# The start of a spectral-filter and gated-FFN kernel: float32 filters, a shared load queue, and batch 0's spectrum in pairs on one side

## The chip, the cores and the metric

The kernel runs on one core of a Trainium2 chip. The metric is the device time of one execution in microseconds (us). The core's engines are named as the profile names them: PE is TensorE, DVE is VectorE, ACT is ScalarE, POOL is GpSimd, SP is SyncE. Loads that SP or ACT issues and loads that POOL issues stand in different DMA queues.

## The reference

The first half is a filter in frequency, the second a feed-forward block with a gate, on all tokens:

```python
X = np.fft.rfft(x, axis=1)                    # x: 8 x 3008 x 256, float32
Y = X * (filt_r + 1j * filt_i)[None, :, :]    # filters: 1505 x 256, float32
y = np.fft.irfft(Y, n=3008, axis=1).reshape(24064, 256)
gate = np.maximum(y @ w_gate, 0.0)            # w_gate, w_val: 256 x 1536
out = (gate * (y @ w_val)) @ w_out            # w_out: 1536 x 256
```

## The kernel before

The transform over 3008 is done as 94 x 32. For each batch there are six stages. **A**: matmuls in float32 with the table `WA` transform over the 94 (`a_bank`, PSUM tile `psA`). Then VectorE transposes 32x32 blocks (the **turn**, in float32 units of two bf16) so that the 32 lie on the partitions (tile `at`). **Forward** (`fwd`): matmuls with table `F2`, 16 small ones into `psX`; there are six forward steps per batch. **Products** (`product`): `psX` times the real filter (`tt`) and times the imaginary filter (`uu`), for batch 0 on VectorE except three pairs on POOL (`ON_POOL`), for which ScalarE first copies `psX` to `xs`. **Inverse** (`inv`): matmuls with the tables `I2t` and `I2u` into four PSUM tiles `psD`; three inverse steps per batch, each on two forward steps. The result is copied to SBUF as bf16 and turned back. **C** (`item_c`): matmuls with the table `M1` back over the 94, into `psY`, copied to `yT`: 512 tokens of y. From there `gv` and `o_part` do the feed-forward block, 47 blocks of 512 tokens, in twelve steps each.

The order is written by hand: each engine runs its instructions in the order of the program. What is looked at here is the front, before the first `gv`. Batch 0 goes through all stages there, and batch 1's stage A goes between them in sixteen **items** (`item`, `a_1`: one matmul into `psA` and its copy to bf16). Everything of the batches 2 to 7 is placed at numbered steps of the feed-forward loop.

Loads in the front. Batch 0's x (3.08 MB) goes on SP's queue, with a few pieces on ACT's, then the tables `F2` and `tabs`. The filters are loaded by POOL, which casts them to bf16 in the DMA: first the rows of an odd partition, which lie backward in memory (`load_back`, 256 elements each, first half of the groups), then the rows of an even partition, long ones of 3072 elements (L234), then the second halves of the backward rows. The two end rows (`load_own_filters`) come before all these; a small copy on POOL (`hold_gpsimd`) makes POOL wait for a late piece of x before it issues the rest. On SP a tiny load called `hold` reads one element block of the imaginary filter: SP waits there until those filter rows have landed, and only then issues batch 1's x into the buffers of batch 0's x. A DMA on SP's or POOL's queue uses one of eight semaphores, so each also waits for the landing of the one eight before it. After its products POOL issues the weights (`load_vg`, `load_o`), copies `M1`, and multiplies the imaginary filter by the table `conj` for the later batches.

Layout of batch 0's spectrum. The copies of `psD` (L464) write a bf16 tile `DS0` in groups of four: for one column index c, four values that are two neighbours in the 32 and two column halves. The turn (`turn_d`, `turn_pairs`, L306) reads and writes two float32 units that are neighbours. `d_rows` then hands strided columns of `D0` to TensorE as weights.

```python
copy(dst[:, k:k + 3:2, :, g:g + 2].rearrange("p m e f -> p m f e"),   # L464
     psD[c].rearrange("p m (f e) -> p m f e", f=2))
return D0[:, n2 // 2, :, n2 % 2 * 2 + h]                              # d_rows
```

Lines that the text names: L190 x pieces, L234 long filter rows, L241 backward rows, L271 stage A, L283 batch 0's copies of `psA`, L296 the items' copies, L301 batch 1's turns (`turn_a`, single float32 units on both sides), L306 batch 0's turns, L408 forward, L426 and L428 products on POOL and VectorE, L451 inverse, L464 copies of `psD`, L550 `psY`, L567 `gv`, L683 the sign of the imaginary filter. `warm` puts matmuls on a junk tile into TensorE's gaps.

Of the kernel before, what the change touches and what calls it, by code (L numbers as in the profile page):

```python
# [12 lines left out]
FP32 = mybir.dt.float32  # L13
BF16 = mybir.dt.bfloat16
# [15 lines left out]
N1, N2 = 94, 32  # L30
# [5 lines left out]
def _ap(t, offset_elems, ap_list):  # L36
    return dataclasses.replace(
        t, offset=t.offset + offset_elems, ap=[list(p) for p in ap_list]
    )
# [77 lines left out]
def kernel(  # L117
# [50 lines left out]
    AS0 = pro.tile([128, 4, N2 // 2, D // 8, 4], BF16)  # L168
    DS0 = AS0.rearrange("p q n c f -> p (q n c f)").rearrange("p (k c f) -> p k c f", c=D // 2, f=4)
    dCb = consts.tile([128, 48, D], BF16)  # L170
    D0 = dCb[:, 0:32, :].rearrange("p n d -> p (n d)").rearrange("p (k c f) -> p k c f", c=D // 2, f=4)
    AS1 = [dCb[:, 32:48, :].rearrange("p n d -> p (n d)").rearrange("p (l c d) -> p l c d", l=NC2, d=D // 2)]
    WF = consts.tile([128, 4, 32], FP32)
    M1 = consts.tile([128, 2, N1], BF16)
# [2 lines left out]
    I2u = pro.tile([128, 2, NG // 2, 64], BF16)  # L177
    Ftr = consts.tile([128, NG // 2, D], BF16)
    Fti = consts.tile([128, NG // 2, D], BF16)
    WgT = consts.tile([128, 2, DFF], BF16)  # L180
    WvT = consts.tile([128, 2, DFF], BF16)
    WoT = consts.tile([128, NFT, D], BF16)
# [10 lines left out]

    WHOLE = ((0, 0, NX2 * D), (1, 0, NX2 * D))
    H = NG // 2
    FILT = ((filt_r, Ftr), (filt_i, Fti))
    tabs = pro.tile([128, tab_h.shape[1]], BF16, tag="tabs", bufs=1)
    conj32 = pro.tile([128, 2], FP32, tag="conj32", bufs=1)
    perm, conj, own = tabs[:, 0:64], tabs[:, 64:66], tabs[96:, 66:578]
# [15 lines left out]
    def make_back_u():  # L215
        nc.scalar.copy(conj32, conj)
        for r in range(2):
            nc.scalar.mul(I2u[:, r], I2t[:, 1 - r], conj32[:, r:r + 1])
# [7 lines left out]
    def load_filters():  # L226

        for src, dst in FILT:
            for c in range(4):
                load_back(src, dst, c, 0, H // 2)  # L230
        for src, dst in FILT:
            for c in range(4):
                r, k1, n = 32 * c, 1 + H * c, H - c // 3
                nc.gpsimd.dma_start(dst[r:r + 31:2, :n, :], _ap(src, k1 * D, [[N1 * D, 16], [1, n * D]]))  # L234
        for src, dst in FILT:
            for c in range(4):
                load_back(src, dst, c, H // 2, H - c // 3)

    def load_back(src, dst, c, g0, g1):
        r, k1 = 32 * c + 1, 1 + H * c + g0  # L240
        nc.gpsimd.dma_start(dst[r:r + 31:2, g0:g1, :],  # L241
                            _ap(src, (N1 - k1) * D, [[N1 * D, 16], [-D, g1 - g0], [1, D]]))
# [61 lines left out]
    def turn_pairs(dst, src):  # L304

        nc.vector.transpose(dst.bitcast(FP32).rearrange("p k c g -> p c k g"),  # L306
                            src.bitcast(FP32).rearrange("p n c g -> p c n g"))
# [13 lines left out]

    def turn_d(h):

        d = slice(h * D // 4, h * D // 4 + D // 4)
        turn_pairs(D0[:, :, d], DS0[:, :, d])

    def store_half(b):
        w = N2 * D // 2
# [86 lines left out]
    def product(b, i, e, k, pool=False):  # L415

        psX = psXs[b, i, e]
        pool_, bufs, dt = (fs, 3, FP32) if b else (pro, 10, BF16)
        p = pool_.tile([128, 2, D], dt, tag=("tt", "uu")[k], bufs=bufs, name=("tt", "uu")[k])
        filt = (Ftr, Fti)[k][:, 2 * i + e, :]  # L420
        filt = dataclasses.replace(filt, ap=[list(filt.ap[0]), [0, 2], list(filt.ap[1])])
        if pool:
            if not k:
                xs[i] = pro.tile([128, 2, D], FP32, tag="xs", bufs=3, name="xs")
                nc.scalar.copy(xs[i], psX)
            nc.gpsimd.tensor_tensor(p, xs[i], filt, op=ALU.mult)  # L426
        else:
            nc.vector.tensor_tensor(p, psX, filt, op=ALU.mult)  # L428
        tus[b, i, e, k] = p
        left[b, i, e] -= 1  # L430
        if not left[b, i, e]:
            done(psX)
# [8 lines left out]
    def inv(b, q):  # L441

        psD = [bank("psD", 2, D) for c in range(4)]
        last = 0 if b else 1
        for m in range(2):
            for k in range(last + 1):
                for r in range(2):
                    for c in range(4):
                        for e in range(2):
                            i = 2 * q + m  # L450
                            nc.tensor.matmul(psD[c][64 * e:64 * e + 64, m],  # L451
                                             (I2t, I2u)[k][32 * c:32 * c + 32, r, 2 * i + e, :],
                                             tus[b, i, e, k][32 * c:32 * c + 32, r],
                                             start=(k == r == 0), stop=(k == last and r == 1),
                                             tile_position=(32 * c, 64 * e))
        dst = sb.tile([128, 8, D], BF16, tag="dsb", bufs=3, name="dsb") if b else DS0
        def out(cs):
            for c in cs:
                copy = nc.vector.tensor_copy if (c % 2 if b else (q, c) in ((1, 3), (2, 0), (2, 1))) else nc.scalar.copy
                if b:  # L460
                    copy(dst[:, c:8:4, :], psD[c])
                else:
                    k, g = 4 * q + c // 2, c % 2 * 2
                    copy(dst[:, k:k + 3:2, :, g:g + 2].rearrange("p m e f -> p m f e"),  # L464
                         psD[c].rearrange("p m (f e) -> p m f e", f=2))
                done(psD[c])
        if not b:
            return out(range(4))

        def rest():  # L470
            out((2, 3))
            for z in range(4):
                nc.sync.dma_start(_ap(Dbuf[b], (64 * (z // 2) + z % 2) * NG * D + 8 * q * D,
                                      [[2 * NG * D, 32], [1, 8 * D]]),
                                  dst[32 * z:32 * z + 32])
        out((0, 1))
        return rest

    def first_b(item):

        def products(i, es=(1, 0)):
            for e in es:
                for k in range(2):
                    product(0, i, e, k, pool=(i, e) in ON_POOL)

        fwd(0, 0)
        warm(2)
        fwd(0, 1)
        make_back_u()
        for i in range(2):  # L490
            products(i, (1,))
        for k in range(2):
            for i in range(2):
                product(0, i, 0, k)
        warm(2)
        fwd(0, 2)
        products(2)
        warm(1)
        fwd(0, 3)
        products(3, (1,))  # L500
        fwd(0, 4)
        item(2)
        products(3, (0,))
        inv(0, 0)
        fwd(0, 5)
        products(4)
        item(2)
        products(5)
        place_own()
        inv(0, 1)  # L510
        item(1)
        inv(0, 2)

    dCs = {}

    def d_rows(b, n2, h):

        if b:
            return dCs[b, n2 // 8][:, n2 % 8, h * 128:(h + 1) * 128]
        return D0[:, n2 // 2, :, n2 % 2 * 2 + h]  # L520

    def load_d(b):

# [20 lines left out]
    def item_c(k, h):  # L544

        if h == 0:
            yTs[k] = sb.tile([128, 2, W], BF16, tag="yT", bufs=3, name="yT")
        psY = bank("psY", W)
        for (o, b, n2, n1, w) in runs(k * W, W):
            nc.tensor.matmul(psY[:, o:o + w],  # L550
                             d_rows(b, n2, h),
                             M1[:, 1, n1:n1 + w] if b == 0 else M1[:NROW, 0, n1:n1 + w],
                             start=True, stop=True)
        dst = yTs[k][:, h]
        if h == 0 or k:
            nc.scalar.copy(dst, psY)  # L556
        else:
            nc.vector.tensor_copy(dst, psY)
        done(psY)
# [74 lines left out]
    nc.vector.memset(XF[1][:, 0:2 * q], 0.0)  # L634
    nc.gpsimd.memset(XF[1][:, 2 * q:], 0.0)
    load_x(0, both, ((0, q, 2 * q),))
    load_x(0, sp, ((0, 2 * q, 4 * q), (1, 0, 2 * q), (1, 2 * q, 4 * q)))
    nc.sync.dma_start(F2, nc.inline_tensor(f2_h, name="dft_f2").ap())
    nc.sync.dma_start(tabs, nc.inline_tensor(tab_h, name="dft_tab").ap())
    for (src, dst) in FILT:  # L640
# [4 lines left out]

    warm(18, 256)
    new_at(0)
    for n2, h in ((0, 0), (0, 1), (4, 0), (4, 1)):
        a_0(n2, 4, h * D // 2, D // 2)
    for p, dq in ((1, 0), (1, 1), (1, 2), (1, 3), (2, 0), (2, 1), (2, 2), (3, 0), (3, 1), (3, 2), (2, 3), (3, 3)):  # L650
        a_0(NC2 * p, NC2, dq * D // 4, D // 4)
        if p == 3:
            turn_0(dq)
    for r in range(2):
        make_back_t(r)
        warm(4 - 2 * r)
    hold = sb.tile([2, 8], BF16, tag="hold", bufs=1)
    nc.sync.dma_start(hold, Fti[96:98, 4, 0:8])
    load_x(1, sp, ((0, 0, 2 * q), (0, 2 * q, 4 * q), (1, 0, 2 * q), (1, 2 * q, 4 * q)))
    items = iter([(p, s, h) for p in range(4) for h in range(2) for s in range(2)])  # L660

# [10 lines left out]
    load_vg(0, DFF // 2)  # L672
    load_vg(DFF // 2, DFF)
    load_o()
    nc.gpsimd.tensor_copy(M1, tabs[:, 578:].rearrange("p (l n) -> p l n", l=2))
    for h in range(2):
        turn_d(h)
# [2 lines left out]
        item_c(0, hh)  # L680
    item(3)
    turn_1(0)
    nc.gpsimd.tensor_scalar(Fti, Fti, conj[:, 0:1], 1.0, op0=ALU.mult, op1=ALU.mult)  # L683
    nc.sync.dma_start(WF, nc.inline_tensor(fold_h, name="dft_fold").ap())
    prologue.close()
    fs = ctx.enter_context(tc.tile_pool(name="fs", bufs=2))
# [86 lines left out]
```

## Time and profile before

| what | value |
|---|---|
| time, median of 3 runs (lowest, highest) | 874.51 us (873.02, 874.99) |
| the profiled execution: time, its span | 875.37 us, 873.6 us |
| granted TensorE clock over the span | 0.995 |
| busy: PE, DVE, ACT, POOL | 852.4, 579.5, 500.2, 462.3 us |
| DMA: moved, mean rate | 101.61 MB, 116 GB/s |
| batch 0's first `psA` starts, last ends (us) | 5.0, 20.4 |
| first product on DVE | 23.3 |
| SP past the hold, first issue of batch 1's x | 24.7 |
| first item's `psA` | 30.2 |
| first turn of batch 0's spectrum | 47.6 |
| first `psY`, first `psV` of the feed-forward block | 52.3, 55.5 |

All starts are counted from the start of the span. A group line of the profile has the line, the engine, the operation, out<-in with shapes and the count; behind the bar the busy time, the mean ns of one; behind the second bar the idle time of the engine before them and what ended it. Instructions on DVE and ACT overlap their neighbours a little, so that the step from one to the next is some 0.1 us (for L464 0.2) shorter than the duration. A float32 matmul shows as two records.

### The profile page before, as it was taken

Reading aid. Unit: us, or ns where it says so; the run is one execution under the profiler, and the core shown is the slowest. Engines: PE = TensorE matmul, PEld = TensorE weight load, DVE = VectorE, ACT = ScalarE, POOL = GpSimd, SP = SyncE. Lnnn points to the kernel's source line nnn. Section 1 sums busy time; section 2 is a strip of 40 time slices with the busy share of each in tenths; the row PEclk is TensorE's granted clock in tenths of the full one; section 3 lists DMA queues with packets and bytes.
Section 4 is the critical chain, followed back from the end, with each engine's and each line's share of the span. In section 5 each row is a group of like instructions: output and inputs, shape, how many; then the busy total and the mean of one; then the engine's idle time right before and its main releaser. Section 6 shows DMA issues by size and latency. Waiting matters only on the chain.

```text
span 873.6 us, 20407 instructions
## 1 busy us (share of the span) xinstructions
PE 852.4 (98%) x7588; PEld 499.8 (57%) x7705; DVE 579.5 (66%) x863; ACT 500.2 (57%) x904; POOL 462.3 (53%) x504
## 2 busy tenths in 40 slices
PE   8799999999999999999999999999999999999997
PEld 4345555665556555566655655566555655666665
DVE  3578875688656876577765777657876588555553
ACT  5685556555665556555555555555565555555552
POOL 7807883277987756958558666667550032000001
PEclk9899999999999999999999999999999999999999
DMA  8976445543584238642396333863445421511111
GB/s 228 237 121 132 132 98 129 143 123 108 157 203 113 55 102 170 182 107 75 92 208 156 85 105 84 207 144 94 96 106 118 113 60 51 124 42 29 38 34 52
DMA packets 101494, 101.61 MB, mean 116 GB/s; under 512 B 21955, under 2 KB 90083, under 8 KB 99858
## 3 DMA queue, kind: packets, MB, share of 16 engines
q1 hardware_dynamic: 81986, 77.96, 35.6%
q0 software_dynamic: 19056, 21.82, 11.7%
q8 instruction: 61, 1.00, 0.5%
q10 hardware_dynamic: 352, 0.52, 0.2%
q14 instruction: 39, 0.32, 0.1%
HBM read 58.23 MB, written 45.88 MB: 119 GB/s over the span
## 4 chain that ended last, share of the span: by engine, by line
PE 94%; ACT 2%; DMA 1%; DVE 1%; issue 1%; SPq 1%; POOL 0%; DVEq 0%
PE psG L567 29%; PE psO L588 28%; PE psV L567 26%; PE psF L373 3%; PE psY L550 3%; PE psA L271 2%; PE psD L451 2%; PE psX L408 1%; ACT AS L464 1%; DMA XF<-in_x_dram 1%; DVE dCb L306 1%; SPq L190 0%; DVE prod L572 0%; DVE tt L428 0%; ACT vsb L570 0%
## 5 line engine op out<-in xcount | busy, mean ns | idle before, releaser
L572 DVE SCALAR_TENSOR_TENSOR prod<-psG,vsb 128x512 bf16<-128x512 f32 x564 | 389.3, 691 | 235.8 <-ACT vsb L570 230.6
L570 ACT CAST vsb<-psV 128x512 bf16<-128x512 f32 x564 | 332.3, 589 | 225.6 <-PE psV L567 161.0
L588 PE MATMUL psO<-WoT,prod 128*128 128x256 bf16 x2256 | 336.5, 273 | 0.8
L567 PE MATMUL psG<-yT,WgT 128*128 128x512 bf16 x1111 | 331.6, 379 | 5.2
L567 PE MATMUL psV<-yT,WvT 128*128 128x512 bf16 x1030 | 314.8, 379 | 0.1
L588 PEld LDWEIGHTS <-prod 128*128 128x128 bf16 x2256 | 220.7, 98 | 143.4
L567 PEld LDWEIGHTS <-WgT 128*128 128x128 bf16 x1128 | 110.0, 98 | 133.4 <-issue 0.2
L438 POOL TENSOR_TENSOR pp<-tt,uu 128x256 bf16<-128x256 f32 x84 | 60.9, 725 | 170.7 <-DVE uu L428 162.5
L567 PEld LDWEIGHTS <-WvT 128*128 128x128 bf16 x1128 | 100.3, 98 | 37.3 <-issue 25.6
L556 ACT CAST yT<-psY 128x512 bf16<-128x512 f32 x93 | 54.5, 586 | 44.1 <-PE psY L550 43.5
L428 DVE TENSOR_TENSOR tt<-psX,Ftr 128x512 f32<-128x512 f32 (+1 forms) x93 | 63.5, 683 | 5.0 <-PE psX L408 4.0
L601 ACT COPY osb<-psO 128x512 f32<-128x512 f32 x92 | 54.1, 588 | 22.1 <-PE psO L588 22.1
L612 POOL DMA_DIRECT2D out_dram<-osb x5 | 2.6, 537 | 119.6 <-ACT osb L601 118.0
L428 DVE TENSOR_TENSOR uu<-psX,Fti 128x512 f32<-128x512 f32 (+1 forms) x93 | 63.2, 681 | 0.0
L439 POOL TENSOR_TENSOR pp<-tt,uu 128x256 bf16<-128x256 f32 x84 | 60.9, 725 | 0.0
L359 POOL TENSOR_TENSOR fold<-XF 128x1024 f32<-128x1024 f32 x24 | 56.4, 2350 | 6.9 <-DMA XF<-in_x_dram 6.4
L360 POOL TENSOR_TENSOR XF<-XF 128x1024 f32<-128x1024 f32 x24 | 56.4, 2350 | 1.9
L263 POOL CAST scr<-prod 128x8 f32<-128x8 bf16 x19 | 3.6, 190 | 92.3 <-DVE prod L572 70.6
L346 POOL DMA_DIRECT2D XF<-in_x_dram x76 | 45.5, 602 | 2.1 <-issue 1.2
L380 ACT CAST asb<-psF 128x512 bf16<-128x512 f32 x48 | 25.8, 589 | 34.5 <-PE psF L373 33.1
L380 DVE CAST asb<-psF 128x512 bf16<-128x512 f32 x48 | 30.9, 686 | 18.2 <-PE psF L373 18.2
L550 PE MATMUL psY<-M,dCb 96*128 96x94 bf16 (+19 forms) x604 | 37.8, 199 | 1.1 <-DVE dCb L306 1.1
(71 smaller groups left out, 474.6 us busy)
## 6 DMA issues: line engine op xcount, KB each, us to landing
Dbuf<-dsb SPq DMA_DIRECT2D x84, 128.0 KB
dCb<-Dbuf SPq DMA_DIRECT2D x56, 192.0 KB
XF<-in_x_dram POOLq DMA_DIRECT2D x38, 256.0 KB, 7.7
Abuf<-asb SPq DMA_DIRECT2D x96, 96.0 KB
at<-Abuf SPq DMA_DIRECT2D x24, 384.0 KB
XF<-in_x_dram SPq DMA_DIRECT2D x31, 256.0 KB
XF<-in_x_dram POOLq DMA_DIRECT2D x76, 96.0 KB, 5.1
out_dram<-osb SPq DMA_DIRECT2D x69, 94.0 KB
```

Source lines behind the costliest of these rows:

```text
L359: tt(t, xp[:, 0:2], xp[:, 2:4], op=ALU.add)
L360: tt(xp[:, 2:4], xp[:, 0:2], xp[:, 2:4], op=ALU.subtract)
L380: copy(asf[:, :, q, :], banks[q])
L428: nc.vector.tensor_tensor(p, psX, filt, op=ALU.mult)
L438: nc.gpsimd.tensor_tensor(p[:, 0], tt[:, 0], uu[:, 1], op=ALU.subtract)
L439: nc.gpsimd.tensor_tensor(p[:, 1], tt[:, 1], uu[:, 0], op=ALU.add)
L550: nc.tensor.matmul(psY[:, o:o + w], d_rows(b, n2, h), M1[:, 1, n1:n1 + w] if b == 0 else M1[:NROW, 0, n1:n1 + w], start=True, stop=True)
L556: nc.scalar.copy(dst, psY)
L567: nc.tensor.matmul(pt[:, :W], w[:, h, ft * 128:(ft + 1) * 128], yt[:, h, :], start=(h == 0), stop=(h == 1))
L570: nc.scalar.copy(vsb, psV[:, :W])
L572: nc.vector.scalar_tensor_tensor(prod, in0=psG[:, :W], scalar=0.0, in1=vsb, op0=ALU.max, op1=ALU.mult)
L588: nc.tensor.matmul(psO[:, t % 2], prods[ft][:, t * 128:(t + 1) * 128], WoT[:, ft, :], start=(ft == 0), stop=(ft == NFT - 1))
```

## The change

There are five parts. The filters for batch 0 are loaded as float32 into two new tiles `F32`, without a cast in the DMA; the bf16 filters for the later batches are made from them on POOL behind the issue of the weights (`cast_filters`), the imaginary one with its sign. The long filter rows move from POOL's queue to SP's, behind the tables; on POOL all backward rows remain. `hold` is gone, and batch 1's x follows on SP behind the long rows. The copies of `psD` write pairs of neighbouring columns; the turn of batch 0's spectrum reads such pairs and writes single float32 units, into the layout that the other batches have, so that `d_rows` falls away. The second half of the first x tile comes in two pieces, and its four stage A matmuls go by those pieces. With less room in SBUF the products have nine buffers instead of ten and `xs` two instead of three, and ScalarE makes `I2u` behind the first two `xs` copies.

```diff
-    D0 = dCb[:, 0:32, :].rearrange("p n d -> p (n d)").rearrange("p (k c f) -> p k c f", c=D // 2, f=4)
+    F32 = [pro.tile([128, NG // 2, D], FP32, name=f"F32{k}") for k in range(2)]
-    FILT = ((filt_r, Ftr), (filt_i, Fti))
+    FILT = ((filt_r, F32[0]), (filt_i, F32[1]))
...
         for src, dst in FILT:
             for c in range(4):
-                load_back(src, dst, c, 0, H // 2)
-        for src, dst in FILT:
-            for c in range(4):
                 r, k1, n = 32 * c, 1 + H * c, H - c // 3
-                nc.gpsimd.dma_start(dst[r:r + 31:2, :n, :], _ap(src, k1 * D, [[N1 * D, 16], [1, n * D]]))
-        for src, dst in FILT:
-            for c in range(4):
-                load_back(src, dst, c, H // 2, H - c // 3)
+                nc.sync.dma_start(dst[r:r + 31:2, :n, :], _ap(src, k1 * D, [[N1 * D, 16], [1, n * D]]))
+        for g0, g1 in ((0, H // 2), (H // 2, H)):
+            for src, dst in FILT:
+                for c in range(4):
+                    load_back(src, dst, c, g0, g1 - g1 // H * (c // 3))
+    def cast_filters():
+        nc.gpsimd.tensor_copy(Ftr, F32[0])
+        nc.gpsimd.tensor_scalar(Fti, F32[1], conj32[:, 0:1], 1.0, op0=ALU.mult, op1=ALU.mult)
...
     def turn_d(h):
-        d = slice(h * D // 4, h * D // 4 + D // 4)
-        turn_pairs(D0[:, :, d], DS0[:, :, d])
+        d = slice(h * D // 2, h * D // 2 + D // 2)
+        e = slice(h * D // 4, h * D // 4 + D // 4)
+        nc.vector.transpose(dCb[:, 0:32, d].bitcast(FP32).rearrange("p (k g) d -> p d k g", g=2),
+                            DS0[:, :, e].bitcast(FP32).rearrange("p n c g -> p c n g"))
...
-        pool_, bufs, dt = (fs, 3, FP32) if b else (pro, 10, BF16)
+        pool_, bufs, dt = (fs, 3, FP32) if b else (pro, 9, BF16)
-        filt = (Ftr, Fti)[k][:, 2 * i + e, :]
+        filt = ((Ftr, Fti) if b else F32)[k][:, 2 * i + e, :]
-                xs[i] = pro.tile([128, 2, D], FP32, tag="xs", bufs=3, name="xs")
+                xs[i] = pro.tile([128, 2, D], FP32, tag="xs", bufs=2, name="xs")
...
-                    copy(dst[:, k:k + 3:2, :, g:g + 2].rearrange("p m e f -> p m f e"),
-                         psD[c].rearrange("p m (f e) -> p m f e", f=2))
+                    copy(dst[:, k:k + 3:2, :, g:g + 2], psD[c].rearrange("p m (e f) -> p m e f", f=2))
...
         fwd(0, 1)
-        make_back_u()
         for i in range(2):
             products(i, (1,))
+        make_back_u()
...
-                             d_rows(b, n2, h),
+                             dCs[b, n2 // 8][:, n2 % 8, h * 128:(h + 1) * 128],
...
-    load_x(0, sp, ((0, 2 * q, 4 * q), (1, 0, 2 * q), (1, 2 * q, 4 * q)))
+    load_x(0, sp, ((0, 2 * q, 3 * q), (0, 3 * q, 4 * q), (1, 0, 2 * q), (1, 2 * q, 4 * q)))
...
-    for n2, h in ((0, 0), (0, 1), (4, 0), (4, 1)):
+    for n2, h in [(n2, h) for n2 in (0, 4, 8, 12) for h in range(2)]:
         a_0(n2, 4, h * D // 2, D // 2)
-    for p, dq in ((1, 0), (1, 1), (1, 2), (1, 3), (2, 0), (2, 1), (2, 2), (3, 0), (3, 1), (3, 2), (2, 3), (3, 3)):
+    for p, dq in ((2, 0), (2, 1), (2, 2), (3, 0), (3, 1), (3, 2), (2, 3), (3, 3)):
...
-    hold = sb.tile([2, 8], BF16, tag="hold", bufs=1)
-    nc.sync.dma_start(hold, Fti[96:98, 4, 0:8])
     load_x(1, sp, ((0, 0, 2 * q), (0, 2 * q, 4 * q), (1, 0, 2 * q), (1, 2 * q, 4 * q)))
...
     load_o()
+    cast_filters()
     nc.gpsimd.tensor_copy(M1, tabs[:, 578:].rearrange("p (l n) -> p l n", l=2))
...
-    nc.gpsimd.tensor_scalar(Fti, Fti, conj[:, 0:1], 1.0, op0=ALU.mult, op1=ALU.mult)
```

More of the change, by code (lines that the diff above doesn't have):

```diff
@@ L512, in first_b @@
         inv(0, 2)
[L514 to L520, printed above, removed]
+    dCs = {(0, z): dCb[:, 8 * z:8 * z + 8, :] for z in range(NZ)}
     def load_d(b):
```

## The prediction

> **What bounds the kernel now.** I read the window table first (stretch; per engine busy us and count; then granted clock, DMA share, GB/s):
>
> ```profile
> 15.00:20.00 5.00, 5.00 (x13) 2.09 (x11) 2.37 (x3) 3.37 (x7) 3.64 (x8) 1.00 0.93 128
> 25.00:30.00 5.00, 1.24 (x33) 0.55 (x33) 5.00 (x9) 1.57 (x4) 4.32 (x4) 0.80 0.95 257
> 30.00:35.00 5.00, 4.81 (x52) 2.22 (x60) 2.04 (x4) 1.17 (x2) 4.94 (x8) 0.51 0.90 341
> 35.00:40.00 5.00, 3.31 (x54) 1.06 (x39) 2.49 (x4) 4.56 (x5) 4.62 (x6) 1.00 1.04 198
> 55.50:873.00 817.50, 806.53 (x7102) 479.17 (x7215) 551.47 (x830) 465.06 (x841) 428.70 (x452) 1.00 0.46 111
> ```
>
> From 55.5 us TensorE is busy 99% (806.53 of 817.5) and the change touches nothing there, so the edit is worth what it moves the start of that stretch. Before it TensorE has holes, and while it starves the granted clock falls to 0.51. The chain of waits in order of time (start, us, what) says which work ends last:
>
> ```profile
> 25.84 4.21 DMA XF<-in_x_dram
> 30.19 3.75 PE psA L271 x4
> 33.94 1.52 PE psD L451 x49
> 35.46 4.72 ACT AS L464 x4
> ...
> 47.64 4.63 DVE dCb L306 x2
> 52.31 0.68 PE psY L550 x12
> 52.99 2.67 PE psA L271 x6
> ```
>
> So: batch 1's x (issued after the hold at 23.8), two items on a slow clock, inverse 0, its copies, later the turns, then the first psY. Third view, the groups by form (count, busy us, mean ns):
>
> ```profile
> L464 ACT CAST AS<-psD 128x512 bf16<-128x512 f32 x9 | 10.8, 1371 | 0.9 <-PE psD L451 0.9
> L283 ACT CAST AS<-psA 128x512 bf16<-128x512 f32 x12 | 7.0, 586 | 4.1 <-PE psA L271 4.1
> L306 DVE STREAM_TRANSPOSE dCb<-AS 128x2048 f32<-128x2048 f32 x2 | 4.6, 2359 | 1.6 <-ACT AS L464 1.6
> L301 DVE STREAM_TRANSPOSE at<-asb 128x512 f32<-128x512 f32 x4 | 4.3, 1081 | 2.4 <-ACT asb L296 2.4
> L464 DVE CAST AS<-psD 128x512 bf16<-128x512 f32 x3 | 3.7, 1313 | 4.0 <-PE psD L451 4.0
> L683 POOL TENSOR_SCALAR Fti<-Fti,tabs 128x3072 bf16<-128x3072 bf16 x1 | 2.8, 2822 | 0.3 <-DVE uu L428 0.3
> ```
>
> L464 and L283 both turn 512 float32 of PSUM into bf16. L464 writes single 2-byte elements 8 bytes apart, L283 pairs: 1371 against 586 ns.
>
> **Part by part.**
>
> *Loads.* Up to 15 us DMA moved 2.30 + 1.73 = 4.03 MB: all of batch 0's x and the tables (3.72), and 0.3 of filters. The new program then owes 1.54 MB of long rows, about 1.4 of backward rows and 0.79 for batch 1's first third. Long rows and x go at the 341 GB/s of 30 to 35: 4.5 and 2.3 us. A backward row, now 1 KB uncast, is not shown; the nearest is the same row with a cast, 60 ns on one of 16 engines, 273 GB/s: 5.1 us. Sum 11.9, end 26.9; I add 1.3 us for the landing (first backward halves: last packets near 16.9, landed 17.9; a little more with two queues): 28.2, against 30.05 before. All at 341 gives 27, all at the 257 of 25 to 30 gives 30. I take 28.2. TensorE is free for it at 26.8, as before.
>
> *Clock.* Two items at full clock are 2 x 0.88 = 1.76 us instead of 3.75. TensorE's hole shrinks from 3.4 us to 1.4. Bounds: 1.76 if the clock holds, 3.75 if it falls again, which moves what follows by up to 2.4 with part of inverse 0. I take the full clock, since the hole is less than half; it is the weaker choice.
>
> *Copies of psD.* Twelve now write pairs, L283's pattern: on ScalarE 0.59 instead of 1.18 apart (4 in 4.72), on VectorE 0.6 instead of 1.22.
>
> *The chain.* Items 28.2 to 30.0 (inverse 0 also needs PSUM banks that VectorE's fourth pair of products frees, at 29.6 before: hidden); inverse 0 to 31.0 (1.0, as the second takes); four copies to 33.4; forward 5 and two items on TensorE to 33.3 beside them; inverse 1 to 34.5; one item to 35.4; inverse 2 to 36.5. VectorE's last six products run from 31.0 to 34.6, hidden; the ninth-buffer limit adds the wait for inverse 0 before two of them, counted there. ScalarE: half-copies 1.3, three copies 1.8, one of an item 0.6 and two copies 1.2 after 33.4: 38.3. So the turns start at 38.3 instead of 47.64. TensorE's eight items take 7.41 from 36.5: 43.9.
>
> *The turns.* They read pairs as before and write 4 bytes at steps of 512. This is not shown. Lower bound: L306 dCb, paired on both sides, 4.63 for both. Upper: L301, unpaired on both sides, 1081 ns for a quarter, 4.3 each, 8.6 for both. L464 is the only row that isolates a side, and there separate writes alone cost double; so I take 8.6. Turns end at 46.9, after the items (43.9), and the first psY comes at 46.9 instead of 52.31: 5.4 us earlier.
> [...]
>
> *At nothing.* Six x pieces instead of three for half a tile: three more SP issues of 0.6. The last piece of x is issued at 10.7 instead of 8.85 and is used at about 15.7; POOL's wait on that tile's end lets backward rows start up to 1.9 later, and their first halves (landed 17.9) are used at 23.3. Uncovered, up to 1.9. Batch 1's x no longer stands behind the hold on SP, but behind eight row DMAs and, eight DMAs back, their landing; that is in the sum. Eight half-width first items cost ScalarE 0.65 for 0.59, under TensorE's 0.88. The inverse table's sign copy moves behind two xs copies, ready at 26.7, used at 30. Float32 filters in VectorE's products: 681 ns whatever the output type, taken as no more; on POOL 1.14 to at most 1.27 (two float32 inputs, L361), six times, 0.8, hidden before 30.0 by starting 1.7 earlier. Weights contiguous instead of strided for psY: loads overlap.
>
> *Casts on POOL.* 3072 elements each, one input: L683 gives 2.82, two-input rows (2350 ns for 1024) at most 7.05. Behind them on POOL stands the copy of M1, for which psY waits. Products end at 30.8, own rows 31.5, six weight DMAs 36.5, casts at 2.9 each 42.3, M1 42.7: hidden under 46.9. At 7.05 M1 comes at 51 and the gain is 1.3. I take 2.9, one input being the nearer row. The weights are issued about 1.6 earlier and land before 50; no wait.
>
> **Sum.** The profiled execution took 875.37 (span 873.6, 1.8 around it), 0.86 above the median of 874.51. 5.4 off gives 870.0 there, 869.1 against the median.
>
> **Rivals.**
> *The turn is paced by its reads.* Then turns end at 42.9, the items (43.9) decide, 8.4 off: 866.1; with the clock down 868.6. For: its read side is the row L306 itself. Against: L464.
> *The filters starve.* POOL's backward rows get the engines only when SP's queue has emptied, and that queue now goes on from x through long rows to batch 1's x. For: the first backward row, issued at 10.4, moved nothing until SP's last tables thinned out at 14. Against: POOL's first tiny rows, issued at 4.9 to 6.5, landed in 3.7 to 4.8 us while SP had 0.77 to 0.92 of the engines. Price: SP's rows end at 15.2 + 4.5 + 9.2 = 28.9, first halves land by 31.6, second by 36; VectorE's last twelve products (0.6) end at 43.2, inverse 2 at 44.2, copies 45.4, unpaired turns 54.0, 1.7 later than now: 876.2, and 877 if the landings come another microsecond later. It decides once the second halves land after about 34.
> [...] No stretch of this trace shows 8 KB pieces and backward rows both waiting for long, so its chance below rests on the two rows just named, one each way.
> *The gain is eaten.* Slow casts give 873.2; with a slow clock and backward rows that come somewhat late besides, nothing is left, 874.5. (A slow clock alone, with unpaired turns, is 3.0 off: 871.5, in the forecast's own range.)
>
> **How the numbers follow.** Forecast (unpaired turn) 0.42, of it 0.15 near 871.5; turn paced by reads 0.28; starvation 0.20; eaten 0.10. 0.2%, 1.75 us, is about what a measurement of this kernel can tell from no change. Faster: 0.42 + 0.28 + 0.03 of the eaten = 0.73; same: 0.07 of the eaten and 0.05 of starvation = 0.12; slower 0.15. Range: from 865.5 (reads pace the turn, clock up, x at 27 to 28) to 875.0 (gain eaten); it leaves out starvation. The forecast's own range is 867.5 to 872.
>
> **What would show it.** Right: batch 1's first psA by 28 to 29 at clock 1.0; L464 near 590 ns; turns from about 38, 4.3 each; first psY near 47, psV near 50. Wrong: turns of 2.3; products that wait for the F32 loads past 25; psY waiting for M1; or a stretch after psV longer than 818.

## The result: slower by 0.35%, and the profile after

The changed kernel takes 877.53 us (median of 9 runs, 876.15 to 880.69), the kernel before beside it 874.92 (9 runs, 873.02 to 876.91). The ratio is 1.0035, with a 95% interval of 1.0018 to 1.0051: 3 us slower, where 5.4 us less were forecast.

The profiled execution of the changed kernel took 879.97 us (span 878.2), 2.4 above its median, so its trace probably shows the loads rather later than they usually come. The stretch after the first `psV` is no longer than before (817.1 us from 61.1 to the end; 818.1 from 55.5 before); all of the loss is in the front. The chain of waits of the kernel after, in order of time (start, us, what):

```profile
14.98 15.58 DMA F<-in_filt_i_dram
30.56 0.28 issue
30.84 8.67 DMA F<-in_filt_i_dram
...
39.64 0.70 DVE uu L433
40.34 0.04 issue
40.38 1.92 PE psD L456 x53
42.30 0.56 PE psX L413 x12
42.86 3.34 PE psA L274 x4
46.20 1.01 PE psD L456 x64
47.21 1.06 PE psA L274 x2
48.26 1.05 PE psD L456 x64
49.31 1.28 DVE AS L469 x2
...
50.69 7.26 DVE dCb L329 x2
57.94 0.05 issue
57.99 0.60 PE psY L548 x11
```

Before, this chain led through batch 1's x. Now it leads through the imaginary filter from 15 to 39.5 us, and everything behind it moves along: the turns start at 50.69 (47.64 before), the first `psY` at 57.99 (52.31). The windows (stretch; busy us and count of PE, PEld, DVE, ACT and POOL; granted clock, DMA share, GB/s):

```profile
25.00:30.00 5.00, 1.81 (x44) 0.54 (x44) 1.12 (x2) 2.60 (x5) 1.04 (x2) 0.86 1.00 251
30.00:35.00 5.00, 2.62 (x26) 1.09 (x26) 2.48 (x4) 0.59 (x1) 4.05 (x4) 0.50 1.05 313
35.00:40.00 5.00, 2.90 (x7) 0.58 (x6) 1.05 (x2) 1.17 (x2) 4.94 (x7) 0.50 0.90 305
40.00:45.00 5.00, 4.62 (x79) 2.69 (x80) 5.00 (x9) 2.15 (x5) 4.96 (x7) 0.50 0.82 126
```

VectorE is busy 5.00 of 5 us from 25 to 30 in the kernel before, and 1.12 here. TensorE waits too, and the granted clock stays at half (0.50) until 45.7. The DMA engines are busy all the time from 25 to 35 (shares of 1.00 and 1.05), yet they move 251 and 313 GB/s; the kernel before moved 341 from 30 to 35 at a share of 0.90. The groups by form (count, busy us, mean ns, and behind the second bar the idle time before them):

```profile
L329 DVE STREAM_TRANSPOSE dCb<-AS 128x2048 f32<-128x2048 f32 x2 | 7.2, 3694 | 0.1
L433 DVE TENSOR_TENSOR uu<-psX,F 128x512 bf16<-128x512 f32 x9 | 6.0, 681 | 8.4 <-DMA F<-in_filt_i_dram 8.4
L469 ACT CAST AS<-psD 128x512 bf16<-128x512 f32 x9 | 4.7, 595 | 4.4 <-PE psD L456 4.3
L240 POOL TENSOR_SCALAR Fti<-F,conj 128x3072 bf16<-128x3072 f32 x1 | 2.8, 2823 | 0.0
```

Products wait 8.4 us for the imaginary filter alone; the copies of `psD` take 595 ns instead of 1371, as they should.

### The profile page after: what moved, and what is told of

It reads as the page before. It is cut to its first block, busy times and chain, and to the rows that moved or that the text cites. A ratio compares the mean times of both kernels' runs of the same rounds, so it can differ in the third digit from the quotient of the medians.

```text
span 878.2 us, 20437 instructions
## 1 busy us (share of the span) xinstructions
PE 854.5 (97%) x7588; PEld 500.1 (57%) x7705; DVE 580.9 (66%) x863; ACT 495.9 (56%) x908; POOL 463.4 (53%) x497
## 4 chain that ended last, share of the span: by engine, by line
PE 91%; DMA 4%; DVE 2%; issue 1%; SPq 1%; POOL 1%; ACT 1%; DVEq 0%; POOLq 0%
PE psG L565 29%; PE psO L586 27%; PE psV L565 26%; PE psF L378 3%; DMA F<-in_filt_i_dram 3%; PE psY L548 3%; PE psD L456 2%; PE psX L413 1%; DVE dCb L329 1%; PE psA L274 1%; SPq L190 1%; DVE prod L570 1%; ACT vsb L568 1%; DMA XF<-in_x_dram 0%; DMA Abuf<-asb 0%
## 5 line engine op out<-in xcount | busy, mean ns | idle before, releaser
L433 DVE TENSOR_TENSOR tt<-psX,Ftr 128x512 f32<-128x512 f32 x84 | 57.3, 682 | 0.0
L433 DVE TENSOR_TENSOR uu<-psX,Fti 128x512 f32<-128x512 f32 x84 | 57.1, 680 | 0.0
L385 DVE CAST asb<-psF 128x512 bf16<-128x512 f32 x48 | 30.9, 686 | 18.2 <-PE psF L378 17.4
```

The source lines that it names most:

```text
L385: copy(asf[:, :, q, :], banks[q])
```

## The experiments

Each ratio is to the kernel before, run beside it on the same chip, with its 95% interval. Rows of the filter are "long" (even partitions) or "backward" (odd ones). "..." in a diff stands for lines of the edit that are left out. At first three theories stood against each other: S, the sharing of the engines between two queues makes the rows late; R, float32 rows are slow by themselves; L, the new layout costs.

**e1_hold**: the kernel after with a hold on SP before batch 1's x.

```diff
+    hold = sb.tile([2, 8], FP32, tag="hold", bufs=1)
+    nc.sync.dma_start(hold, F32[1][96:98, 4, 0:8])
     load_x(1, sp, ((0, 0, 2 * q), (0, 2 * q, 4 * q), (1, 0, 2 * q), (1, 2 * q, 4 * q)))
```

> The changed kernel with the hold put back: SP waits for the imaginary filter's first rows before it issues batch 1's x. Theory S (sharing: POOL's backward rows get one small packet for each 8 to 12 KB piece of SP's queue, and this alone made them late): they share with the long rows until 27 us as now, but no longer with batch 1's x; the last backward row lands near 34 us instead of 39.5, batch 1's x lands after it, near 36, and the first psV comes 2 to 4 us earlier than in the changed kernel, 874 to 876. Rival R (backward rows in float32 on POOL's queue are slow by themselves, each of the last eight waiting for the landing of the one eight before): last landing stays at 39 or later and batch 1's x comes later still, 877.5 to 880.

The ratio is 1.0029 (1.0018 to 1.0040), that of the kernel after. The last filter rows land at 31.1 instead of 39.5, but x is then issued from 30.4, and the items' first `psA` starts at 35.88. Holding x back only exchanges one late load for another. So which load is late follows from who shares the engines, but keeping x apart wins nothing.

**e2_pool_rows**: e1 with all filter rows, float32, on POOL's queue in the order of the kernel before.

```diff
-                nc.sync.dma_start(dst[r:r + 31:2, :n, :], _ap(src, k1 * D, [[N1 * D, 16], [1, n * D]]))
+                nc.gpsimd.dma_start(dst[r:r + 31:2, :n, :], _ap(src, k1 * D, [[N1 * D, 16], [1, n * D]]))
...
```

> As the run with the hold, and the long rows back on POOL's queue between the two halves of the backward rows, as in the kernel before; the filters stay float32 and the layout stays the new one. Theory S: with one queue at a time the rows land by about 27 us as in the kernel before, and the front is that of before with fast copies (4.8 us off the path) and slower turns (7.25 instead of 4.63 us): first psV at 53 to 54.5, 873 to 874.5. Rival R: backward rows still land after 35, 877 or more. Rival L (the layout is what costs): 877 as the changed kernel.

The ratio is 1.0023 (1.0014 to 1.0031). One queue works at a time, and it is still slow: batch 1's x is issued from 29.5 (24.7 before), the last rows land at 31.1 (26.75).

**e6_one_queue**: the kernel after with all filter rows on SP's queue, backward ones whole, before batch 1's x; POOL no longer waits for a piece of x.

```diff
-        nc.gpsimd.dma_start(dst[r:r + 31:2, g0:g1, :],
+        nc.sync.dma_start(dst[r:r + 31:2, g0:g1, :],
...
```

> The changed kernel with all filter rows on SP's queue, backward rows whole (16 DMAs), before batch 1's x; POOL loads only the end rows. The same bytes in float32, one queue. Theory S: no sharing, the rows land by 25 to 27 us, batch 1's first x by 28 to 30, first psV at 49 to 52, 868 to 871. Rival R (float32 rows of 1 KB are slow as such): rows land after 32, 875 or more.

The ratio is 1.0039 (1.0026 to 1.0053). From 18 to 29 us nothing but filter rows moves, on one queue, with the engines full (the profile's DMA queues: packets, MB, share of 16 engines):

```profile
DMA packets 1456, 2.39 MB, mean 217 GB/s; under 512 B 194, under 2 KB 1358, under 8 KB 1358
...
q1 hardware_dynamic: 1455, 2.37, 106.8%
```

So 217 GB/s is all that these rows get even alone. Theory S falls.

**e3_before_layout**: the kernel before with the new layout (copies, turn, weights) and nothing else.

```diff
-                    copy(dst[:, k:k + 3:2, :, g:g + 2].rearrange("p m e f -> p m f e"),
-                         psD[c].rearrange("p m (f e) -> p m f e", f=2))
+                    copy(dst[:, k:k + 3:2, :, g:g + 2], psD[c].rearrange("p m (e f) -> p m e f", f=2))
...
```

> The kernel before with only the new layout of batch 0's spectrum: pairs written by the copies, single float32 units written by the turn. Theory S: copies near 590 ns instead of 1371, both turns 7.25 us instead of 4.63, first psV 1 to 2 us earlier than before, 873 to 874. Rival L: the turns' 2.6 us come on top and nothing is won by the copies, 877 to 878.

The ratio is 0.9974 (0.9962 to 0.9985): 2.3 us faster. On its chain of waits stand

```profile
32.52 3.75 PE psA L270 x4
...
44.73 7.23 DVE dCb L325 x2
```

From the items' first `psA` to the turns it is 12.2 us instead of 17.4, and the turns take 7.23 instead of 4.63: 5.2 saved, 2.6 given back. Theory L falls.

**e8_x_pieces**: the kernel before with the smaller x pieces and the order of stage A that goes with them.

```diff
-    load_x(0, sp, ((0, 2 * q, 4 * q), (1, 0, 2 * q), (1, 2 * q, 4 * q)))
+    load_x(0, sp, ((0, 2 * q, 3 * q), (0, 3 * q, 4 * q), (1, 0, 2 * q), (1, 2 * q, 4 * q)))
...
```

> The kernel before with the smaller x pieces and the order of the first stage A matmuls of the kernel after, and nothing else. If the pieces delay stage A as the kernel after showed (last psA 21.66 instead of 20.41): +1.2 us or somewhat more, 0.14 to 0.2%. If the delay is hidden, as the prediction had it: within 0.1%. It also gives the price of the float32 rows by difference: the run with all rows in float32 on POOL's queue (+2.0 us) had the layout (-2.3), these pieces, and the float32 rows.

The ratio is 1.0018 (1.0002 to 1.0034): about 1.6 us, with 0.2 to 3 possible. POOL waits for the end of that tile, so all of its filter DMAs start later: the first backward row is issued at 11.4 instead of 10.4, and SP comes to the first piece of batch 1's x at 27.4 instead of 24.7 in the profiled execution (879.5 us, the slowest of its 12 runs). Part of that is scatter: with the loads of the kernel before, e3's profiled execution came to x at 26.3.

What makes float32 rows slow was then asked with a new theory, G: a DMA that writes into one group of 32 partitions (all filter rows do; a piece of x goes to every fourth of 128) is slow by where it writes: a float32 row of 12288 bytes took 0.84 us in the median in the kernel after, 14.6 GB/s, a piece of x of 8192 bytes 0.309 in the kernel before, 26.5 GB/s. F says that such rows are slow wherever they go.

**e7_spread**: the kernel after, a long-row DMA carrying 32 rows into every fourth partition.

```diff
-                nc.sync.dma_start(dst[r:r + 31:2, :n, :], _ap(src, k1 * D, [[N1 * D, 16], [1, n * D]]))
+                nc.sync.dma_start(dst[2 * r::4, :H - 1, :],
+                                  _ap(src, (1 + r * N1) * D, [[H * D, 4], [2 * N1 * D, 8], [1, (H - 1) * D]]))
...
```

> The kernel after, in which the long filter rows on SP's queue are grouped otherwise: instead of 16 rows for 16 partitions of one group of 32, a DMA carries 32 rows for every fourth partition of all 128, as the pieces of x do; the twelfth group of 256 goes in a small DMA of its own. Same bytes, same queue, same place. Theory G (a DMA that writes into one group of 32 partitions gets only part of the way into SBUF, so float32 rows, with twice the bytes of cast ones, run at 12 to 16 GB/s on each DMA engine where a piece of x, spread over all partitions, runs at 26): rows of 11264 bytes take 0.43 to 0.5 us instead of the 0.73 to 0.95 of the kernel after, the first halves of the backward rows land by 27 to 28, the second by 35 to 36 instead of 39.5, the time falls by 2 to 3 us against the kernel after (from 0.1% faster to 0.1% slower than the kernel before). Theory F (float32 filter rows are slow wherever they go): a row takes 0.7 to 0.9 and the time is that of the kernel after, 0.35% above the kernel before. Theory S (only the sharing between the two queues counts): as F, since the queues share as before.

The ratio is 1.0118 (1.0099 to 1.0137): far slower, which neither theory expected. From 24 to 27 us the queues are:

```profile
q1 hardware_dynamic: 24, 0.22, 19.4%
q0 software_dynamic: 73, 0.14, 17.0%
```

SP's queue keeps 19.4% of 16 engines busy, 3.1 of them, while x waits behind it. The source's outermost dimension has 4 steps (`[H * D, 4]`); with 16 (the kernel after, 77.5% and 27.4% on the two queues) or 32 (e11 below, 66.2 and 35.5) outermost the engines were full. No run changed that number alone, so the four steps are a likely cause, not a shown one. The rows themselves took 0.44 us there, but with so few engines running that doesn't decide between G and F.

**e9_layout_spread**: e3 with the same 32-row DMAs for the cast long rows on POOL's queue.

```diff
-                nc.gpsimd.dma_start(dst[r:r + 31:2, :n, :], _ap(src, k1 * D, [[N1 * D, 16], [1, n * D]]))
+                nc.gpsimd.dma_start(dst[2 * r::4, :H - 1, :],
+                                    _ap(src, (1 + r * N1) * D, [[H * D, 4], [2 * N1 * D, 8], [1, (H - 1) * D]]))
...
```

> The kernel before with the new layout of the spectrum (0.26% faster by itself), and the long filter rows, still cast and on POOL's queue, grouped over all 128 partitions. Theory G with half the bytes: the long rows of 0.77 to 1.03 us in the kernel before go, all take about 0.45 (they read 12 KB, as fast as an engine reads x), the last filter rows land 1 to 2 us earlier than 26.7, and the time is 0.35 to 0.5% below the kernel before. If cast rows are limited by their reading alone: as the layout alone, 0.2 to 0.3% below.

The ratio is 1.0043 (1.0024 to 1.0062), 0.7% above e3. Its trace doesn't show why: it is that of the fastest of its 12 executions (875.84 us; the slowest took 883.58), and there the queue was behind e3's only from 18 to 22 us (65 and 123 GB/s against 148 and 165). The same four outermost steps are a likely reason, but not a shown one. As a test of G it was lost.

**e10_x_group**: the kernel before, each piece of batch 1's x into 32 neighbouring partitions.

```diff
-                engs[m % len(engs)].dma_start(XF[c][m:m + 4 * rows - 3:4, c0:c1],
+                engs[m % len(engs)].dma_start((XF[c][32 * m:32 * m + rows, c0:c1] if group else XF[c][m:m + 4 * rows - 3:4, c0:c1]),
...
```

> The kernel before, in which the pieces of batch 1's x go into 32 neighbouring partitions instead of every fourth one; same source, sizes, number of rows and order (batch 1's rows then stand in wrong partitions, so its part of the output is not the reference's). Theory G (writing into one group of 32 partitions is slow): pieces of 8192 bytes, 0.309 us each before, take 0.5 to 0.62 while they run alone, the first third of batch 1's x lands at 32 to 33 instead of 30.05, and since the chain runs through it, the time rises by 2 to 3 us (0.2 to 0.35%). Theory F (float32 filter rows are slow for their size or their source): still 0.309 us and the time of the kernel before.

The queues of the kernel before from 27 to 35 us, then of this one from 27 to 38, batch 1's x nearly alone in both:

```profile
DMA packets 482, 2.64 MB, mean 330 GB/s; under 512 B 161, under 2 KB 161, under 8 KB 161
...
q1 hardware_dynamic: 481, 2.62, 92.1%
```

```profile
DMA packets 470, 2.54 MB, mean 231 GB/s; under 512 B 155, under 2 KB 161, under 8 KB 161
...
q1 hardware_dynamic: 461, 2.52, 100.8%
```

Same source, same 8 KB pieces, same queue: 22.2 GB/s for each busy engine (2.62 MB / (0.921 x 16 x 8 us)) become 14.2, the median piece 0.558 us instead of 0.309. Only the partitions differ, so the slow rate of G is shown on x. That the filter rows owe theirs to the same cause, and not to F, is for e11 to show. The price was not 2 to 3 us: 1.0007 (0.9997 to 1.0016). Only the 0.79 MB of the first third stand on the chain, 2.3 us at 341 GB/s and 3.4 at 231; so the step is 1.1 us. The profiled executions show it, 5.41 us from the third piece's issue to its landing instead of 4.21, but there it was issued 0.6 earlier.

**e11_rows_spread**: the kernel after with 32-row DMAs into every fourth partition and one step in the source, for long and backward rows.

```diff
-                nc.sync.dma_start(dst[r:r + 31:2, :n, :], _ap(src, k1 * D, [[N1 * D, 16], [1, n * D]]))
+                nc.sync.dma_start(dst[2 * r::4, :H - 1, :],
+                                  _ap(src, (1 + r * H) * D, [[N1 // 2 * D, 32], [1, (H - 1) * D]]))
...
```

> The kernel after, in which every filter row DMA carries 32 rows into every fourth of the 128 partitions with one step in the source, so that all engines take part, on the same two queues (the rows come from other places of the filters, so the products have wrong filter values; bytes, sizes and counts are nearly the same). Theory G: long rows of 11264 bytes take 0.43 to 0.5 us instead of 0.84 per 12288, the backward packets of 4096 bytes 0.16 to 0.2 instead of 0.25 to 0.3, the last filter rows land by 28 to 31 instead of 39.5, the first psV comes 4 to 6 us before the kernel after's, and the time is 0.2 to 0.4% below the kernel before (its layout gives -2.3, its smaller x pieces +1.6). Theory F: rows of 0.75 to 0.95, and the kernel after's time, 0.35% above the kernel before. If sharing between the two queues is what counts: rows in between, and second halves still after 35.

The ratio is 0.9957 (0.9940 to 0.9974), 0.78% below that of the kernel after. What differs is where the rows are written, and with it which rows go together, in 16 row DMAs instead of 24; bytes and queues are nearly the same. The queues of the kernel after from 18 to 27 us, then of this one from 18 to 24:

```profile
q1 hardware_dynamic: 303, 1.57, 77.5%
q0 software_dynamic: 274, 0.57, 27.4%
```

```profile
q1 hardware_dynamic: 313, 1.52, 66.2%
q0 software_dynamic: 309, 0.79, 35.5%
```

For each busy engine that is 14.1 and 14.4 GB/s in the kernel after, 23.9 and 23.2 here. A row of 11264 bytes, which both kernels load uncast, took 0.84 us in the median there and 0.45 here, so F falls: these rows aren't slow by themselves. What the smaller number of DMAs adds to the 0.78% was not measured; e10, which changed no number, shows a like step in rate. The last rows land at 28.1 instead of 39.5. Its chain of waits:

```profile
29.22 3.34 PE psA L276 x4
32.57 1.05 PE psD L458 x64
...
40.71 7.29 DVE dCb L331 x2
48.05 0.60 PE psY L550 x11
```

**e12_no_hold**: the kernel before without its hold.

```diff
-    nc.sync.dma_start(hold, Fti[96:98, 4, 0:8])
```

> The kernel before without the hold on SP, and nothing else: cast rows on POOL's queue beside batch 1's x on SP's. Theory S for cast rows: the second halves, 25.4 to 26.8 before, land at 31 to 34, batch 1's first third at 24 to 27 instead of 30.05, the products end 4 to 6 us later, the copies of psD come after them, and the time is 0 to 2 us above the kernel before. If cast rows keep their pace beside x: second halves by 28, and a gain of 2 to 3 us, since the chain ran through x.

The ratio is 1.0020 (1.0008 to 1.0033): the hold is worth about 1.8 us in the kernel before. In the profiled execution, the fastest of its 12 (874.60 us), the last rows land at 32.4 instead of 26.75 and the products wait for them; the items on TensorE, which stand behind forward steps, start at 29.75, hardly earlier. From 24 to 32 us both queues have data:

```profile
q0 software_dynamic: 935, 0.57, 49.0%
q1 hardware_dynamic: 234, 1.25, 45.9%
```

**e5_pair_writes**: the kernel before; its copies of `psD` write pairs and read PSUM apart, everything else stays.

```diff
-                    copy(dst[:, k:k + 3:2, :, g:g + 2].rearrange("p m e f -> p m f e"),
-                         psD[c].rearrange("p m (f e) -> p m f e", f=2))
+                    copy(dst[:, k:k + 3:2, :, g:g + 2], psD[c].rearrange("p m (f e) -> p m e f", f=2))
```

> The kernel before, in which the copies of psD write pairs of the two column halves and read them from PSUM 256 apart; turns stay paired on both sides; the columns of the spectrum come in another order, which is not undone, so that the halves' neighbours are exchanged in the output of batch 0. If a copy's cost is set by its separate 2-byte writes: 0.59 instead of 1.37 us per copy with turns of 2.36, 4 to 5 us faster than the kernel before (0.45 to 0.6%), that is 2.6 us better than the new layout with its turns of 3.7. If reading PSUM apart costs as much as writing apart: 1.2 to 1.4 us per copy and the time of the kernel before.

The ratio is 0.9941 (0.9922 to 0.9960): 5.2 us faster than the kernel before, and better than the new layout. (Against what the expectation says, no columns change places: every value goes where it went, in another order of walking.)

```profile
L464 ACT CAST AS<-psD 128x512 bf16<-128x512 f32 x9 | 4.7, 596 | 1.7 <-PE psD L451 1.6
L306 DVE STREAM_TRANSPOSE dCb<-AS 128x2048 f32<-128x2048 f32 x2 | 4.6, 2332 | 0.1
```

Reading two halves that lie 512 bytes apart in PSUM costs ScalarE next to nothing (596 ns against L283's 586), and the turn stays at 2.33 us. On its chain the turns are gone: inverse 2 is followed by eight items on TensorE (42.87, 7.06 us) and `psY` at 49.93.

**e13_early_hold**: e5 with the hold on the real filter.

```diff
-    nc.sync.dma_start(hold, Fti[96:98, 4, 0:8])
+    nc.sync.dma_start(hold, Ftr[96:98, 4, 0:8])
```

> The kernel before with the copies of psD that read PSUM apart (0.6% faster than before by itself), and with the hold on the real filter's last long row instead of the imaginary one's: batch 1's x is issued at about 22 instead of 25.4. If x is the late one in that kernel: the items' first psA at 28 to 29.5 instead of 31.5 and another 1 to 2 us off (0.7 to 0.8% below the kernel before). If the last filter rows then become late by as much: no change against 0.6%.

The ratio is 0.9937 (0.9920 to 0.9954), not to be told from e5's. In the profiled execution the items started at 29.35 instead of 31.53 and the first `psV` came at 49.92 instead of 53.09, but the medians don't show that step: single executions of one kernel lie up to 4.6 us apart here (the kernel after, 876.15 to 880.69). Between the traces of the two kernels, of e5 and of e13 the front differs and the stretch from the first `psV` on hardly does (817.1 to 818.3 us). Both this and e5 beat both kernels.

## Why the prediction was wrong, by its own steps

**Loads: the step that failed.** It took long rows at 341 GB/s, the rate of batch 1's x, and backward rows at 273. Both ran at 14.1 to 14.4 GB/s for each engine, some 230 for all sixteen. The first third of x and the first halves of the imaginary filter landed at 33.8 and 30.6 instead of by 28.2, and the second halves, which the sum had done by then, at 39.5; they decided. The rows that it took were no near ones: x is spread over all partitions, the filter rows go 16 at a time into one group of 32. The kernel before hid this, because its casting DMAs write half the bytes: its long rows read 12 KB in 0.473 us in the median, as fast as an engine reads x (26 GB/s), where the uncast rows took 0.84. The 273 GB/s for backward rows were counted in the same way, by what a casting DMA reads. Taking the cast away saved no reading and doubled the writing where writing is slow. With nearly the same bytes spread over all partitions (e11) this term comes out within its bounds of 27 to 30: 385 GB/s from 18 to 24 us, first item at 29.2.
Loads into one group of 32 partitions did not all run at one rate: 217 GB/s for all filter rows on one queue (e6), 231 for x (e10), and 253 for the rows on POOL's queue alone (e2, from 18 to 25 us). No run shows what sets it.

**The chain behind it: right in its order, and in its length by luck.** From the first item to the first `psY` the prediction had 28.2 to 46.9, 18.7 us. In e11, where the filters come in time, it is 29.22 to 48.05, 18.8. But two errors cancel there: up to the turns it is 11.5 us instead of 10.1, since the first two items took 3.34 and not 1.76, and the turns took 7.3 instead of 8.6. In the kernel after it is 24.2, since inverse 0 waits for the last product until 40.38. The copies at 595 ns are right. The turn, taken at 4.3 us each and bounded by 2.3 below, took 3.69: writing single units costs, but less than on both sides; so neither the forecast's price nor the rival's held.

**Clock: wrong**, as the weaker choice. TensorE's hole was 3.7 us and not 1.4, and the clock stayed at half from 28.6 to 45.7: the first two items took 3.75 us. With the loads in time (e11) it fell too, to half from 28.6 to 32.0 (0.86 over 25 to 30, 0.80 over 30 to 35).

**At nothing: one edit failed.** Smaller x pieces cost about 1.6 us (e8, loosely known), not nothing: all filter rows stand behind that tile on POOL, so their last ones move too, not only the first halves that the text looked at. Float32 products (681 ns; POOL 1.26 us), the casts (2.74 and 2.82), `M1` (copied at 49.7, before the turns end), and contiguous weights (98 ns for one load up to 60 us, 115 strided) cost what was said.

**The rivals.** "The filters starve" gave 876.2 to 877, near the 877.53 measured, but not for its reason. POOL's queue is not shut out while SP's has work: it held 27.4% of the engines beside SP's 77.5% in the kernel after, and 49.0 beside 45.9 in e12. The sharing put the second halves late (31.1 in e1, where x is held, 39.5 without the hold), but the time was lost by the rate of all rows. Its deciding point, second halves landing after about 34, was right. "The gain is eaten" had the slow clock and somewhat late rows, but its slow casts didn't come, and the rows were far later.

**The parts, measured alone.** Layout -2.3 us, x pieces +1.6, and float32 rows on one queue +2.7 (e2's +2.0, less the other two). The rest up to the kernel after's +3.0, about 1, is the new order on two queues; e2 and the kernel after overlap in their intervals, so that last term is not settled. The sum takes the parts as independent, and each is known to a microsecond or so at best. With its rows spread the whole change is 0.43% or 3.8 us faster than the kernel before (e11), 6.8 better than as it stands; but e11 takes its rows from other places of the filters, and e7, with the right ones, ran on about 3 engines.

## What to carry to other kernels

Before a DMA's rate is borrowed from another, compare where both write: a load that goes 16 or 32 rows at a time into one group of 32 partitions ran here at about 0.6 of the rate of one spread over all 128 (14 against 22 to 24 GB/s for each busy engine). The cast to bf16 in the DMA halved the bytes that are written; without it a long row took 0.84 us in the median instead of 0.473, so dropping a cast can cost time where writing is slow. And where a copy out of PSUM has to change an order, let it read apart and write neighbours: here a copy took 596 ns instead of 1371, and this alone brought 5.2 us, the new layout 2.3.

## What the runs showed of the hardware that was not expected

- The same 8 KB pieces took 0.558 us in the median into 32 neighbouring partitions and 0.309 into every fourth one (e10 against the kernel before).
- A DMA of 32 rows whose source had 4 as its outermost dimension ran on about 3 engines (e7: 19.4% of 16).
- ScalarE's copy of 512 float32 took 596 ns with reads 512 bytes apart in PSUM and paired writes, 1371 ns with single 2-byte writes 8 bytes apart in SBUF.
- A turn of 2048 float32 units took 2.33 us paired on both sides, 3.69 with paired reads and single writes.
